# The first attention of a fused attention and gated-MLP kernel: division by the softmax sums after P times V instead of before

## The chip, the cores and the metric

One core of one Trainium2 chip runs the whole program. The metric is the device time of one execution in microseconds (us). The profile is of one execution; its time stands beside its span.

## What is computed

For 8 batches, 8 heads of width 64 and 576 positions: causal attention with a window of 128 positions and a bias that falls with distance, then a gated MLP whose second half is normalized and mixed along the sequence. Cut to what matters:

```python
scores = q @ k.T / 8;  rel = pos[:, None] - pos[None, :]
scores = where((rel >= 0) & (rel < 128), scores - slope[h] * abs(rel), -1e9)
p = exp(scores - max(scores));  attn = p / (sum(p) + 1e-9);  x = attn @ v
h = relu(x @ w_in);  u, g = halves(h);  g = layer_norm(g)
out = (u * (w_spatial @ g + b_spatial)) @ w_out
```

## The kernel before, in words

Two heads make a pair, so a batch has four pairs; 576 query positions make five tiles (t), the last of 64. Inputs are float32. Later batches split P and V into two f16 words and transpose P by DMA. The first 25 tiles, the "raw" ones (`RAW`: all four pairs of batch 0 and the first pair of batch 1), do everything in f32 on TensorE. This is the code that the change touches.

A raw tile goes through `raw_tile` and `raw_rest`: scores of both heads into PSUM (L508); bias, mask and row maximum on VectorE (L514, a custom operation and a read of its accumulator); Exp on ScalarE with the row sum taken by its accumulator (L519); the addition of 1e-9 and the reciprocal (L525, L526), once for two pairs in batch 0; P times reciprocal, one instruction a head, on ScalarE (L540) or VectorE (L541); transposes of P against an identity (L550); a copy from PSUM to `pq` (L281); and x, transposed, as V (64 columns of weights a head, one head in each half of the array) times moving P (L568). Its high f16 word is a copy (L281) and its low word a subtraction (L576), both into `xt`. V was scaled on GpSimd (L490), in place. A pair of batch 0 has the buffers `prob`, `pq` by its slot. `gated` then works on `xt`: v units (L765, L787), u units (L817), spatial mixing (L838), output (L864); its call `first(t)` weaves the raw tiles of batch 0 and the preparation of the weights (`words`, L298 to L314; `win_split`, L341 to L346) between its v units. The weight words pass through a buffer `wa` into `wx`.

No order is written by hand. `Plan.add` collects operations with an engine, a cost, a due time and the buffer parts that they read and write; `either` gives two engines to choose from. `Plan.order` simulates the five queues with these costs, sends each `either` to the engine that it expects to end it first, takes the earliest due time of what is ready, and so sets the order of every engine's queue. The hardware then runs each queue in that order, each instruction when its inputs are there. A change of costs or dependences in the raw tiles can thus reorder all queues.

Of the kernel before, what the change touches and what calls it, by code (L numbers as in the profile page):

```python
# [13 lines left out]
I32 = mybir.dt.int32  # L14
# [18 lines left out]
class Buf:  # L33
# [107 lines left out]
def attn_gmlp_kernel(ctx, tc, qk, v, w_in, w_spT, b_sp, w_out, outT):  # L141
# [83 lines left out]
    rstat = fixed([P, 8, 8], F32, "rstat")  # L225
# [5 lines left out]
    def xcols(x, a, c0, c1):  # L231
        return parts(x, c0, c1, 32, (a,))
# [55 lines left out]
    def words(src, n, x, due):  # L288


        a = plan.buf(work, "wa", 2, [P, DH], F32)
        low = lambda: src()[:, :, 0].bitcast(U32)
        high = lambda: src()[:, :, 1]
        ai, xi, xu = lambda: a().bitcast(I32), lambda: x().bitcast(I32), lambda: x().bitcast(U32)
        A, X, W = (a, 0), (x, 0), (src, 0)

        def f():
            nc.scalar.activation(a(), high().bitcast(F32), AF.Abs)  # L298
        plan.add("ACT", act(n), due, f, [W], [A])

        def f():
            nc.vector.tensor_scalar(a(), a(), TINY, CLAMP, ALU.max, ALU.min)
        plan.add("DVE", dve(n, True), due, f, [A], [A])

        def f():
            nc.vector.tensor_scalar(xi(), ai(), 0x07FFFFFF, 3, ALU.bitwise_and, ALU.logical_shift_left)
        plan.add("DVE", dve(n, True), due + 1, f, [A], [X])
# [166 lines left out]
    def values(b, due):  # L474
# [11 lines left out]

        for p in range(NP):
            if (b, p) in RAW:
                def f(p=p):
                    nc.gpsimd.tensor_scalar(vb()[:, p], vb()[:, p], am()[:, 5:6], None, ALU.mult)  # L490
                plan.add("POOL", 800, due + 9011 + p, f, [(vb, p), (am, 1)], [(vb, p)])
        return vb, am

    def raw_tile(b, p, t, raw, vb, xt, slot, due, sums=None):

        m, k0, k1 = min(P, S - t * P), max(0, (t - 1) * P), min(S, (t + 1) * P)
        n, c0 = k1 - k0, P if t == 0 else 0
# [11 lines left out]
        plan.add("PE", SWITCH // 2 + pe(*[4 * n]), due, f, [(raw, k) for k in range(k0 // P, t + 1)], [(sc[j], 0) for j in range(2)])
        for j in range(2):  # L510
            h = 2 * p + j

            def f(j=j, h=h):
                nc.vector.tensor_tensor_reduce(pr[j](), sc[j]()[:m, 0, :n], tabs[h]()[:m, c0:c0 + n], -0.125, 3e38,  # L514
                                               ALU.add, ALU.min, st(NM, j))
            plan.add("DVE", dve(n), due + 300, f, [(sc[j], 0), (tabs[h], 0)], cols[j] + [(rstat, row)])

            def f(j=j):
                nc.scalar.activation(pr[j](), pr[j](), AF.Exp, bias=st(NM, j), scale=-1.0, accum_out=st(SM, j))  # L519
# [11 lines left out]
    def raw_rest(b, p, t, vb, xt, slot, due, row):  # L531
# [46 lines left out]
        if t == NQ - 1:  # L578
            tail(xt, due + 2200)
# [397 lines left out]
```

## Time and profile before

| | |
|---|---|
| median of 3 runs (lowest to highest) | 603.81 us (602.73 to 604.26) |
| the profiled execution, its span | 603.51 us, 601.8 us |
| TensorE (PE) busy | 556.0 us, 92% |
| VectorE (DVE) busy | 510.3 us, 85% |
| ScalarE (ACT) busy | 432.9 us, 72% |
| GpSimd (POOL) busy | 61.3 us, 10% |
| mean DMA rate | 132 GB/s |

PEld is TensorE's loading of weights, which can overlap its matmuls; SPq is the queue that issues DMAs. Busy times by engine are the union of its instructions. A row names the source line, then what is written, an arrow, and what is read. A matmul in f32 shows as two records, a transpose as one.

### The profile page before, as it was taken

To read this page: it belongs to the slowest core of one execution; us is meant where nothing else is said; L and a number is where in the kernel's file an instruction comes from. 1 tells how busy PE (TensorE), PEld (TensorE's weight loads), DVE (VectorE), ACT (ScalarE), POOL (GpSimd) and SP (SyncE) were. 2 spreads that over 40 slices of the span, in tenths; PEclk is the share of its full clock that TensorE was granted. 3 is DMA by queue.
4 is the path that set the end of the run, shared out by engine and by line. 5 is a ranking of instruction groups with operands and counts; after the bars stand their busy time and mean duration, and the time that the engine had idled before them with its cause. 6 is when DMAs were issued, how large, how long until landed. Compare 5 with 4: busy or idle time off the path is not lost. (4 is left out here: it accounts for less than half of the span.)

```text
span 601.8 us, 14776 instructions
## 1 busy us (share of the span) xinstructions
PE 556.0 (92%) x5359; PEld 415.1 (69%) x5359; DVE 510.3 (85%) x1813; ACT 432.9 (72%) x1361; POOL 61.3 (10%) x113
## 2 busy tenths in 40 slices
PE   4567797998799999999999999999999999999997
PEld 2245454777558885788667876888578867896786
DVE  6979999999899799988998989989998899954640
ACT  5678988797888678868886888767985877743212
POOL 2501041100010101010011002000101001000100
PEclk9988878999999999999999999999999999999999
DMA  8930421189944584587856693568555654451002
GB/s 279 377 123 3 154 90 36 48 173 243 209 119 96 177 196 111 121 207 148 169 115 150 128 214 93 124 169 185 129 106 120 167 111 80 80 121 39 1 11 70
DMA packets 149997, 79.64 MB, mean 132 GB/s; under 512 B 129826, under 2 KB 140066, under 8 KB 149924
## 3 DMA queue, kind: packets, MB, share of 16 engines
q1 hardware_dynamic: 149924, 78.70, 54.1%
q8 instruction: 42, 0.69, 0.5%
q14 instruction: 31, 0.25, 0.1%
HBM read 37.13 MB, written 9.44 MB: 77 GB/s over the span
## 5 line engine op out<-in xcount | busy, mean ns | idle before, releaser
L621 ACT ACTIVATE prob<-prob,stat 128x256 f32<-128x256 f32 (+2 forms) x270 | 124.7, 465 | 27.3 <-DVE stat L615 27.3
L864 PE MATMUL m<-gs,wout 128*128 128x288 f32 x768 | 112.7, 301 | 7.0 <-DVE o L872 5.1
L838 PE MATMUL m<-wsp,vn 128*128 128x288 f16 x768 | 114.0, 287 | 0.1
L864 PEld LDWEIGHTS m<-gs,wout 128*128 128x128 f32 x768 | 103.9, 188 | 11.3 <-DVE o L872 5.9
L661 DVE SCALAR_TENSOR_TENSOR pq<-prob,stat,pq 128x128 f16<-128x128 f32 x270 | 106.7, 434 | 3.1 <-ACT pq L656 2.3
L656 ACT ACTIVATE pq<-prob,stat 128x128 f16<-128x128 f32 x270 | 105.1, 465 | 3.9 <-ACT prob L621 2.3
L817 PE MATMUL m<-xt,win 128*128 128x288 f16 x768 | 101.5, 288 | 0.5 <-ACT vt L285 0.4
L817 PEld LDWEIGHTS <-win 128*128 128x128 f16 x768 | 74.6, 98 | 23.9 <-issue 4.5
L765 PE MATMUL m<-win,xt 128*128 128x512 f16 x384 | 87.2, 384 | 1.0 <-DVE o L872 0.9
L838 PEld LDWEIGHTS <-vn 128*128 128x128 f16 x768 | 72.3, 98 | 22.5 <-issue 4.0
L615 DVE CUSTOM_DVE_ANT_0 prob<-s,tab 128x256 f32<-128x256 f32 (+2 forms) x222 | 74.0, 377 | 0.0
L765 PEld LDWEIGHTS <-xt 128*128 128x128 f16 x384 | 36.8, 99 | 45.0 <-issue 3.3
L735 POOL TENSOR_TENSOR st<-st,nhalf 128x1 f32<-128x1 f32 (+1 forms) x40 | 26.1, 654 | 356.1 <-DVE st L731 356.1
L621 ACT ACTIVATION_READ_ACCUMULATOR prob<-prob,stat 128x1 f32 (+1 forms) x270 | 51.0, 189 | 0.0
L871 ACT ACTIVATE o<-m,am 128x288 f32<-128x288 f32 x38 | 18.8, 499 | 41.5 <-PE m L864 26.2
L846 DVE TENSOR_TENSOR u<-m,u 128x288 f32<-128x288 f32 x64 | 28.7, 449 | 21.6 <-PE m L838 21.3
L700 PE MATMUL x<-pt,vh 128*64 128x256 f16 (+6 forms) x756 | 42.5, 229 | 2.0 <-DMA pt<-pq 2.0
L285 ACT ACTIVATE u<-m 128x288 f32<-128x288 f32 x51 | 20.4, 403 | 32.9 <-PE m L817 32.4
L604 PE MATMUL s<-qkraw 64*64 64x192 f32 (+2 forms) x876 | 40.6, 310 | 0.0
L700 PEld LDWEIGHTS <-vh 128*64 128x64 f16 x756 | 32.6, 110 | 9.6 <-issue 9.4
L700 PE MATMUL x<-pt,vl 128*64 128x256 f16 (+6 forms) x378 | 35.7, 228 | 0.0
L604 PEld LDWEIGHTS s<-qkraw 64*64 64x64 f32 x876 | 30.0, 133 | 6.4 <-issue 5.3
(151 smaller groups left out, 819.1 us busy)
## 6 DMA issues: line engine op xcount, KB each, us to landing
qkraw<-in_qk_dram SPq DMA_DIRECT2D x28, 576.0 KB, 4.2
vb<-in_v_dram SPq DMA_DIRECT2D x32, 320.0 KB, 4.7
out_dram<-o SPq DMA_DIRECT2D x64, 144.0 KB, 2.2
vn<-in_w_in_dram SPq DMA_DIRECT2D x8, 512.0 KB, 7.1
pt<-in_w_out_dram SPq DMA_DIRECT2D x4, 512.0 KB, 4.4
gs<-in_w_spT_dram SPq DMA_DIRECT2D x4, 288.0 KB, 6.6
qkraw<-in_qk_dram SPq DMA_DIRECT2D x3, 320.0 KB, 8.2
pt<-pq SPq DMA_TRANSPOSE x54, 4.7
```

The lines of the kernel that those rows point to most:

```text
L604: nc.tensor.matmul(sc[k][j]()[out, i, a - k0:z - k0], raw()[rows, 0, q:q + D], raw()[rows, 1, a:z], start=True, stop=True, skip_group_chec ...
L615: nc.vector.tensor_tensor_reduce(pt(), sc()[:m, i, :n], tabs[h]()[:m, c0:c0 + n], -0.125, 3e38, ALU.add, ALU.min, st()[:m, NM, j, t:t + 1])
L621: nc.scalar.activation(pt(), pt(), AF.Exp, bias=st()[:m, NM, j, t:t + 1], scale=-1.0, accum_out=st()[:m, SM, j, t:t + 1])
L656: nc.scalar.activation(pq[j]()[:m, 0, cs], prob[j]()[:m, cs], AF.Copy, scale=st()[:m, RC, j, t:t + 1])
L661: nc.vector.scalar_tensor_tensor(pq[j]()[:m, 1, cs], prob[j]()[:m, cs], st()[:m, RC, j, t:t + 1], pq[j]()[:m, 0, cs], ALU.mult, ALU.subtract)
L700: nc.tensor.matmul(xp()[j * D:(j + 1) * D, x0:x0 + n], l()[:, kt, j * D:(j + 1) * D], rhs[:, o:o + n], start=j not in seen, stop=False, sk ...
L735: nc.gpsimd.tensor_tensor(st()[:m, 11:12], st()[:m, 10:11], nhalf()[:m], ALU.pow)
L765: nc.tensor.matmul(pt(), xt[c]()[:, X0[a] + t * P:X0[a] + (t + 1) * P], win()[:, c, w, DH:DF], start=(n == 0), stop=(n == 3 * NC_ - 1))
L817: nc.tensor.matmul(pt()[:, :HS], win()[:, c, w, d * P:(d + 1) * P], xt[c]()[:, X0[a] + hf * HS:X0[a] + (hf + 1) * HS], start=(n == 0), sto ...
L838: nc.tensor.matmul(pt()[:, :HS], l, r, start=(n == 0), stop=(n == len(ops) - 1))
L846: nc.vector.tensor_tensor(u(), pt()[:, :HS], u(), ALU.mult)
L864: nc.tensor.matmul(pt()[:, :HS], wout()[:, d, w, e * P:(e + 1) * P], gs[d]()[:, a, :], start=(n == 0), stop=(n == 3 * ND - 1))
```

## The change

P is no longer scaled. Exp loses its accumulator. The unscaled P is transposed as before, but is then the weights of TensorE (128 columns, one head after the other), and the moving operand is V with a 65th column of ones, a new tile `vones` that GpSimd fills (L502, L504). So x comes out with queries along partitions, and its 65th column is the row sum. `raw_tiles` takes one pair or, in batch 0, two: it adds 1e-9 to the sums (L578), takes reciprocals (L579), multiplies x by them (L586), transposes x on TensorE (L591, one transpose a pair) into the PSUM tile that it came from, and copies and subtracts for both pairs at once (L291, L600). `xt` holds two pairs in each of three buffers instead of one in each of six. `wa` is gone: the absolute value of the weight words (L307) is written to `wx` directly.

```diff
     def words(src, n, x, due):
-        a = plan.buf(work, "wa", 2, [P, DH], F32)
...
+            nc.scalar.activation(x(), high().bitcast(F32), AF.Abs)
+        plan.add("ACT", act(n), due, f, [W], [X])
...
     def values(b, due):
-                    nc.gpsimd.tensor_scalar(vb()[:, p], vb()[:, p], am()[:, 5:6], None, ALU.mult)
+                vo = vones[p] = plan.buf(work, "vones", 4, [P, NQ, 2, D + 1], F32)
+                    nc.gpsimd.tensor_scalar(vo()[:, :, :, 0:D], vb()[:, p].rearrange("q a (j d) -> q a j d", j=2), am()[:, 5:6], None, ALU.mult)
+                plan.add("POOL", 150, due, lambda vo=vo: nc.gpsimd.memset(vo()[:, :, :, D:D + 1], 1.0), (), [(vo, 1)])
...
-    def raw_tile(b, p, t, raw, vb, xt, slot, due, sums=None):
+    def raw_tiles(b, t, raws, vos, xts, slots, due):
...
-                nc.scalar.activation(pr[j](), pr[j](), AF.Exp, bias=st(NM, j), scale=-1.0, accum_out=st(SM, j))
+                    nc.scalar.activation(pr(i, j), pr(i, j), AF.Exp, bias=nm(j), scale=-1.0)
...
-            plan.either([("ACT", act(n, 1), lambda j=j: nc.scalar.activation(pr[j](), pr[j](), AF.Copy, scale=st(RC, j))),
-                         ("DVE", dve(n, True), lambda j=j: nc.vector.tensor_scalar(pr[j](), pr[j](), st(RC, j), None, ALU.mult))],
...
-                    nc.tensor.matmul(xp()[j * D:(j + 1) * D, :m], vb()[:w, p, k // P, j * D:(j + 1) * D], pf(w, c, c + m),
+                        nc.tensor.matmul(xp()[:m, o:o + D + 1], pf(w, c, c + m), vos[i]()[:w, k_ // P, j, :],
...
+            nc.vector.tensor_scalar(TM(), xv()[:, :, D:D + 1], 1e-9, None, ALU.add)
+            nc.vector.reciprocal(RC(), TM())
+        plan.add("DVE", 220, due + 1900, f, XP, [(rstat, (row, 2))])
...
+            nc.vector.tensor_tensor(xn().rearrange("p (j d) -> p j d", j=J), xv()[:, :, 0:D], RC().to_broadcast([m, J, D]), ALU.mult)
+        plan.add("DVE", dve(J * D), due + 1950, f, XP + [(rstat, (row, 2))], ncols)
...
+                nc.tensor.transpose(xp()[:, i * m:(i + 1) * m], xn()[:, i * P:(i + 1) * P], ident()[:m, :m])
+        plan.add("PE", SWITCH // 2 + pe(*[2 * m] * len(raws)), due + 2000, f, ncols + [(ident, 0)], XP)
...
+        copy(len(raws) * m, lambda: (xt(0), xT()), due + 2100, XP, xh)
+            nc.vector.tensor_tensor(xt(1), xT(), xt(0), ALU.subtract)
...
-        xt = plan.buf(work, "xt", 6, [P, 2 * S + R], F16)
+            held[b, p // 2] = plan.buf(work, "xt", 3, [P, 2, 2 * S + R], F16)
```

TensorE's queue after the first tiles' transposes, before (x is the PSUM tile of P times V, s that of the scores, m that of the transposes):

```order
L568 MATMUL x<-pq_95,vb 64x128 x2
L508 MATMUL s_66<-qkraw 128x256
L508 MATMUL s_67<-qkraw 128x256
L568 MATMUL x<-pq_96,vb 64x128 x2
L568 MATMUL x<-pq_95,vb 64x128 x2
L508 MATMUL s_68<-pt 128x256
L508 MATMUL s_69<-pt 128x256
L568 MATMUL x<-pq_96,vb 64x128 x2
```

And the same place of the change:

```order
L568 MATMUL x<-vones,pq_95 128x65 x2
L568 MATMUL x<-vones,pq_96 128x65 x2
L568 MATMUL x<-vones,pq_95 128x65 x2
L568 MATMUL x<-vones,pq_96 128x65 x2
L591 MATMUL x<-ident,prob_93 128x128 x4
L526 MATMUL s_66<-qkraw 128x256
L526 MATMUL s_67<-qkraw 128x256
L526 MATMUL s_68<-pt 128x256
L526 MATMUL s_69<-pt 128x256
```

The scores of the second tile's pairs 2 and 3 stood between the x matmuls of the first tile; they now stand behind all of these and behind the transposes of x.

VectorE's queue in the change, over the same work (wx are the words of the weights; L586 and L600 are of pairs 0 and 1 of the first tile, L578 and L579 of pairs 2 and 3):

```order
L586 TENSOR_TENSOR prob_93<-x,rstat 128x256
L319 SCALAR_TENSOR_TENSOR wx<-vn_125,wx 128x512
L311 TENSOR_SCALAR wx<-wx 128x512
L323 SCALAR_TENSOR_TENSOR wx<-vn_125,wx 128x512
L315 TENSOR_SCALAR wx<-wx 128x512
L600 TENSOR_TENSOR xt<-x,xt 128x2x128
L319 SCALAR_TENSOR_TENSOR wx<-vn_129,wx 128x512
L311 TENSOR_SCALAR wx<-wx 128x512
L323 SCALAR_TENSOR_TENSOR wx<-vn_129,wx 128x512
L315 TENSOR_SCALAR wx<-wx 128x512
L578 TENSOR_SCALAR rstat<-x 128x4
L579 RECIPROCAL rstat<-rstat 128x4
```

The subtraction of pairs 0 and 1 (L600) now stands ahead of words of the weights and of the sums and the normalization of pairs 2 and 3; before, VectorE's only step on x was one subtraction a pair (L576).

## Rows read from the trace of the kernel before

**Rows 1.** The table of stages, over the whole span: start and end in us, length, then busy us (and instructions) of PE, PEld, DVE, ACT and POOL, the clock granted to TensorE as a share of 2.4 GHz, the DMA engines' busy share, GB/s.

```profile
0.00:45.00 45.00, 24.86 (x131) 14.70 (x132) 34.01 (x141) 29.74 (x96) 12.00 (x18) 0.95 0.73 261
45.00:105.00 60.00, 48.84 (x324) 29.11 (x323) 55.63 (x186) 52.77 (x150) 12.09 (x22) 0.83 0.22 71
105.00:150.00 45.00, 42.49 (x474) 32.87 (x472) 44.20 (x174) 36.39 (x127) 3.79 (x8) 1.00 0.67 152
150.00:300.00 150.00, 144.76 (x1530) 110.39 (x1531) 135.64 (x488) 119.53 (x386) 11.05 (x23) 1.00 0.70 157
300.00:450.00 150.00, 148.32 (x1543) 112.34 (x1542) 138.62 (x492) 118.57 (x378) 13.55 (x26) 1.00 0.64 142
450.00:560.00 110.00, 109.17 (x1073) 83.71 (x1071) 87.69 (x301) 68.56 (x213) 7.70 (x14) 1.00 0.45 98
560.00:602.00 42.00, 37.56 (x295) 31.98 (x293) 14.51 (x36) 7.37 (x16) 1.14 (x2) 0.98 0.09 29
```

**Rows 2.** What PE waited for between 45 and 105 us: waiting line, releaser, us in total, times, longest.

```profile
PE m L433 <- DVE wide L431: 3.4, 1, 3.4
PE s L550 <- ACT prob L540: 3.4, 1, 3.4
...
PE m L550 <- ACT prob L540: 3.0, 1, 3.0
```

**Rows 3.** The table of stages for three short stretches; columns as in rows 1.

```profile
45.00:47.50 2.50, 2.50 (x15) 2.17 (x16) 1.53 (x6) 1.41 (x4) 1.28 (x5) 0.50 0.07 13
...
77.50:80.00 2.50, 2.47 (x14) 1.71 (x14) 2.39 (x7) 1.78 (x5) 0.00 (x0) 0.50 0.07 13
...
97.50:120.00 22.50, 22.50 (x208) 16.40 (x207) 21.15 (x73) 16.94 (x55) 2.94 (x6) 0.97 0.20 55
```

**Rows 4.** Instructions by line and shape from 0 to 110 us: count, then busy us and mean ns of one, then idle time of the engine before them and what ended it.

```profile
L514 DVE CUSTOM_DVE_ANT_0 prob<-s,tab 128x256 f32<-128x256 f32 x30 | 11.8, 416 | 1.0 <-PE s L508 0.5 <-PE m L550 0.3
...
L519 ACT ACTIVATION_READ_ACCUMULATOR prob<-prob,rstat 128x1 f32 x40 | 7.6, 190 | 0.0
L540 ACT ACTIVATE prob<-prob,rstat 128x256 f32<-128x256 f32 x15 | 6.8, 497 | 0.8 <-DVE rstat L526 0.8
...
L576 DVE TENSOR_TENSOR xt<-x,xt 128x128 f16<-128x128 f32 x20 | 5.5, 281 | 1.8 <-ACT xt L281 1.8
...
L541 DVE TENSOR_SCALAR prob<-prob,rstat 128x256 f32<-128x256 f32 x15 | 4.4, 347 | 0.0
...
L281 DVE COPY pq<-m 128x512 f32<-128x512 f32 x4 | 2.7, 688 | 1.0 <-PE m L550 1.0
...
L541 DVE TENSOR_SCALAR prob<-prob,rstat 128x128 f32<-128x128 f32 x9 | 2.0, 281 | 0.1
...
L541 DVE TENSOR_SCALAR prob<-prob,rstat 64x192 f32<-64x192 f32 x6 | 1.5, 306 | 0.0
...
L525 DVE TENSOR_SCALAR rstat<-rstat 128x4 f32<-128x4 f32 x8 | 1.3, 167 | 3.0 <-ACT prob L519 3.0
...
L576 DVE TENSOR_TENSOR xt<-x,xt 128x64 f16<-128x64 f32 x4 | 0.8, 216 | 0.0
```

**Rows 5.** The timeline from 28 to 62 us: start, us, engine, line, operation, how many in a row.

```profile
28.36 0.40 DVE L514 CUSTOM_DVE_ANT_0 prob<-s,tab 128x256 f32<-128x256 f32 x1
...
30.90 0.51 ACT L519 ACTIVATE prob<-prob,rstat 128x256 f32<-128x256 f32 x1
...
31.41 0.50 ACT L519 ACTIVATE prob<-prob,rstat 128x256 f32<-128x256 f32 x1
...
34.78 1.09 PE L550 MATMUL m<-ident,prob 128*128 128x128 f32 x8
...
48.31 2.73 DVE L346 SCALAR_TENSOR_TENSOR win<-wx,ham,win 128x512 f16<-128x512 f32 x4
...
52.04 0.76 DVE L302 TENSOR_SCALAR wa<-wa 128x512 f32<-128x512 f32 x2
...
56.82 1.71 ACT L540 ACTIVATE prob<-prob,rstat 128x256 f32<-128x256 f32 x4 [0.51 <-DVE rstat L526]
```

**Rows 6.** The timeline of PE alone from 56 to 120 us.

```profile
57.38 2.10 PE L550 MATMUL m<-ident,prob 128*128 128x128 f32 x8 [3.04 <-ACT prob L540]
...
70.91 1.09 PE L568 MATMUL x<-pq,vb 128*64 128x128 f32 x16
...
107.69 0.54 PE L838 MATMUL m<-wsp,vn 128*128 128x288 f16 x3
```

**Rows 7.** The table of stages for line L568 alone: start and end, length, busy us (and records) of PE and PEld, granted clock, DMA share, GB/s.

```profile
45.00:105.00 60.00, 10.23 (x116) 6.86 (x116) 0.83 0.22 71
```

**Rows 8.** The chain that ended last, in order of time: start, us, engine, tile and line, records.

```profile
509.19 1.72 PE m L838 x14
```

**Rows 9.** The timeline from 0 to 45 us.

```profile
1.18 0.10 POOL L381 MEMSET wam<- 128x8 f32 x1
...
4.01 1.67 PE L508 MATMUL s<-qkraw 64*128 64x128 f32 x8 [4.01 <-DMA qkraw<-in_qk_dram]
...
16.62 8.44 POOL L490 TENSOR_SCALAR vb<-vb,am 128x640 f32<-128x640 f32 x4 [0.73 <-ACT pq L281]
...
19.31 1.23 PE L508 MATMUL s<-qkraw 64*128 64x256 f32 x4
...
23.72 1.23 PE L508 MATMUL s<-pt 64*128 64x256 f32 x4
```

More of the change, by code (lines that the diff above doesn't have):

```diff
@@ L509, in raw_tile @@
[L509 to L518, printed above, removed]
-                nc.scalar.activation(pr[j](), pr[j](), AF.Exp, bias=st(NM, j), scale=-1.0, accum_out=st(SM, j))
-            plan.add("ACT", act(n, 2), due + 600, f, cols[j] + [(rstat, row)], cols[j] + [(rstat, row)])
@@ L522, in raw_tile @@
-        r0, r1 = sums or (row, row + 1)
-        def f():
-            nc.vector.tensor_scalar(rstat()[:m, r0:r1, TM:TM + 2], rstat()[:m, r0:r1, SM:SM + 2], 1e-9, None, ALU.add)
-            nc.vector.reciprocal(rstat()[:m, r0:r1, RC:RC + 2], rstat()[:m, r0:r1, TM:TM + 2])
-        if sums is None or row == r1 - 1:
-            plan.add("DVE", 190, due + 900, f, [(rstat, r) for r in range(r0, r1)], [(rstat, r) for r in range(r0, r1)])
-        return lambda: raw_rest(b, p, t, vb, xt, slot, due, row)
@@ new lines, in raw_tiles @@
+        J = 2 * len(raws)
+        xv = lambda: xp()[:m, 0:J * (D + 1)].rearrange("p (j e) -> p j e", j=J)
+        XP = [(xp, i) for i in pairs]
+        TM, RC = [lambda c=c: rstat()[:m, row, c:c + J].rearrange("p (j o) -> p j o", o=1) for c in (4, 8)]
+        due += 1500 * (len(raws) - 1)
+        def f():
+            nc.vector.tensor_scalar(TM(), xv()[:, :, D:D + 1], 1e-9, None, ALU.add)
+            nc.vector.reciprocal(RC(), TM())
+        plan.add("DVE", 220, due + 1900, f, XP, [(rstat, (row, 2))])
@@ L578, in raw_rest @@
+        plan.add("DVE", dve(len(raws) * m), due + 2200, f, XP + xh, xl)
         if t == NQ - 1:
-            tail(xt, due + 2200)
+            for x in xts:
+                tail(x, due + 2300)
     def clear():
@@ L908, in attn_gmlp_kernel @@
     mixing_weights(FIRST + 8000)
-    x0 = [plan.buf(work, "xt", 6, [P, 2 * S + R], F16) for _ in range(NP)]
+    x0 = [xbuf(0, p) for p in range(NP)]
     wu = []
@@ L913, in first @@
         for p0 in range(0, NP, 2) if t < NQ else ():
[L914 to L916 removed]
+            raw_tiles(0, t, loads[p0:p0 + 2], [vones0[p] for p in (p0, p0 + 1)], x0[p0:p0 + 2], [p0, p0 + 1], 2000 + t * 6500 + p0 * 1500)
         if t == 1:
```

163 lines of the change are left out of this document (90 added, 73 removed).

## The prediction

> **What bounds the kernel now.** I read the table of stages first [rows 1]. From 150 us on TensorE (PE) is busy 439.8 of 452 us at a granted clock of 0.98 to 1.00, and the work there is not touched. The 25 tiles of the first attention (five of each of batch 0's four head pairs, five of batch 1's first pair) lie before 115 us. So a gain or a loss has to arise in the first 150 us, and it reaches the end only as far as PE then starts its long full stretch earlier or later. Before 45 us PE is idle 20.1 us, from 45 to 105 us 11.2 us, from 105 to 150 us 2.5 us. VectorE (DVE) is busy 55.6 of 60 us and then 44.2 of 45: from 45 to 150 us it is the engine with the least room, 95%, while ScalarE (ACT) has 52.8 of 60 and 36.4 of 45.
>
> The waits of PE between 45 and 105 us come second [rows 2]: 6.4 us in two waits of the transposes L550 for the scaling L540 on ACT, and 3.4 us for the small matmul L433, whose input is queued on DVE behind ACT's work. Third comes the clock [rows 3]: after such idle time PE runs at 1.2 GHz (0.50), and from 97.5 to 120 us it is busy all the time at 0.97 of 2.4 GHz. Whatever is added on PE there has no cover.
>
> **Part by part: DVE.** Fifty scalings of P by the reciprocal go. The table by shape [rows 4] has 30 of them on DVE, 4.4 + 2.0 + 1.5 = 7.9 us, and the order of the instructions shows that 30 stood on DVE and 20 on ACT. The 25 subtractions L576 (20 of 281 ns, 5 of 216 ns: 6.7 us) become 15 for two pairs or one. Ten of these have two pairs: eight have 256 elements and two 128; five have one pair, four of 128 and one of 64. For 256 elements from PSUM the nearest row is L514 at 416 ns, so 8 x 0.42 + 6 x 0.28 + 0.22 = 5.3 us: 1.4 us less. New are 15 normalizations L586, ten of 256 elements and five of 128: 10 x 0.42 + 5 x 0.28 = 5.6 us more. The addition and the reciprocal keep their count of 15, but the addition now reads four scattered PSUM words; bounds are 0 (as L525's 167 ns) and 0.25 us each (as L514's 416 ns); I take 0.05, 0.8 us. The planner, which sees less work on ACT, also moves shared operations off DVE: two P copies (688 ns each, 1.4 us) and six small casts late in batch 0, for which I take 1.2 us: 288 of the 512 elements that cost 688 ns would make 2.3 us, and 0 is the other end, as they may be off the path. A relu leaves DVE and a weight split comes to it, which cancel. Sum for DVE: -7.9 - 1.4 + 5.6 + 0.8 - 2.6 = **-5.5 us**.
>
> **ACT.** Twenty scalings go (15 of them 6.8 us). Fifty reads of the accumulator go too; 40 are booked with 7.6 us, but they overlap: two Exp with a read start 0.51 us apart, four L540 of the same shape take 1.71 us, 0.43 each [rows 5], so a read costs 0.08 us and fifty cost 4. Pair casts replace single ones (about -3), two P copies come (+1.2). ACT loses some 14 us. It isn't the bound after 45 us, so I count nothing for it beyond what it does to waits: the 3.0 us that DVE's L525 waited for Exp [rows 4] go, since the sums now come from PE. In their place L578 and L586 wait for P times V; I let these cancel, with ends of -3 and +3.
>
> **PE.** The trace has no f32 matmul with 128 columns of weights and 65 moving. Now eight matmuls of two tiles (16 records, two a matmul) take 1.09 us [rows 6], 0.136 us each, two heads side by side in the array's halves. The heads now follow each other. Nearest for a full f32 load is the transpose L550: 1.09 us for eight records at full clock [rows 5], 0.136 us a record, 2.10 us at half clock [rows 6]. Two records make 0.27 us a matmul at full clock and 0.53 at half; the other bound is 0.136, if loads hide. I take 0.27, so 0.136 more a matmul, and 0.136 for each new transpose of x; at half clock it is twice that. From 45 to 105 us run 116 of L568's 180 records, 58 of 90 matmuls [rows 7]. Twenty of them, of the last query tile, load 64 columns and count half, so 48, and with some 14 transposes 62 x 0.136 = 8.4 us at full clock against 11.2 us of idle time: hidden if it falls into that idle time, and I count it so. Behind 97.5 us the last three tiles of batch 1 run on a full PE: two with five instructions and one of half that, 12.5 x 0.136 = **+1.7 us**, not hidden.
>
> The Trainium skill, page "TensorE: Matmul & The Clock Gate", section "Part 3: Packing small matmuls", says that weight loads overlap matmuls in flight only when their row groups differ; these are all full-height. By that each of 180 records would also pay for streaming its 65 columns, at least 27 ns, 4.9 us more on PE, and the slow rival below would be likelier. The trace disagrees for f16: 14 full-height matmuls of 288 columns take 1.72 us [rows 8], 123 ns each, about their columns alone, so loads are hidden there. No row shows it for f32 with so few columns.
>
> **The first tile's queue.** Before, PE computed scores for pairs 2 and 3 of the second tile at 19.31 and 23.72 us, between the x matmuls that wait for POOL's four scalings of V (16.62 to 25.06 us) [rows 9]. Now those scores stand behind all four x and behind the transposes of x. The second transpose needs a DVE normalization that itself is queued behind the subtraction of pairs 0 and 1, hence behind the first transpose, hence behind the last V: I trace the scores to about 30 us and their softmax, which DVE began at 28.36 us [rows 5], to some 2 us later. Against that, POOL starts about 0.8 us earlier (six reads and a scaling less on ACT's path to the scale of V), and ACT saves five scalings and 16 reads, 3.5 us, on its way to what L433 waits for. I take 0 at 45 us, with ends -2 and +2.
>
> **At no cost.** POOL's memsets of the ones column (0.10 us each, as L381) come before the mask tables, but the first scores wait for their load until 4.01 us [rows 9]. The V loads of batch 2 move from SP's later queue to right behind the w_in loads, since V's buffer is free once POOL has written the new tile; DMA is busy 22% after 45 us [rows 1], which covers them; if it did not, batch 1's Q and K loads behind them would be late next. Without its own buffer the first step of the weight words waits until the split has freed the target (L346, 48.31 to 51.04 us); DVE only comes to those words at 52.04 us [rows 5]. If that cover goes, one ACT and one DVE step, about 1.1 us, is late once.
>
> **Sum.** The profiled execution took 603.51 us (span 601.8, and 1.7 around it), 0.3 below the median of 603.81. 603.5 - 5.5 (DVE) + 1.7 (PE, uncovered) + 0 = **599.7 us**.
>
> **Rivals.**
> 1. *Everything shows.* PE's transposes no longer wait for sums, reciprocal and scaling, the added PE work falls into idle time, and DVE's 3.0 us of waiting for Exp go without replacement: 603.5 - 5.5 - 3.0 = 595.0. For it: the 6.4 us of PE waits on L540. Against: PE full from 97.5 us.
> 2. *Hidden.* PE's backlog takes it: 8.4 us more in a stretch with 11.2 us idle leaves 2.8 us; where steps that depend on each other can't use more than half of the 11.2 us, 2.8 us stay uncovered, and with the 1.7 they use up most of the 5.5: 603.5 - 5.5 + 2.8 + 1.7 = 602.5. For it: 100% PE from 97.5 to 120 us.
> 3. *Slower: PE becomes the bound between 45 and 105 us.* Place: the f32 loads at L568. It decides from 11.2 / 62 = 0.18 us more an instruction. At half clock the price is 0.27, 16.8 us in all, 5.6 more than the idle time; with the 1.7 behind it and no gain from DVE, which then waits for PE, 603.5 + 5.6 + 1.7 = 610.8. Midway between no loss and that, 607. For it: 45 to 47.5 and 77.5 to 80 us run at 0.50 [rows 3], and PE now also waits in order for DVE's normalization 15 times. Against: fewer long waits should leave less half clock.
>
> **How the numbers follow.** Forecast (gain of 2 to 6 us) 0.36; rival 1 0.14; rival 2 0.20; rival 3 0.30. About 0.3%, 1.8 us, is what a measurement of this kernel can tell from no change: faster 0.50, same 0.20, slower 0.30. The range runs from 594.5 (just past rival 1) to 608 (most of rival 3): the dear end of rival 3 and a gain above rival 1 are left out. The forecast's own range is 597.5 to 602.
>
> **What would show it.** Right: L541, L540 and the reads gone, DVE's busy time 0 to 150 us down by about 5 us, L568 at about 0.27 us a matmul at full clock, PE idle from 45 to 105 us below 5 us, and the first matmuls of the spatial mixing (L838 before) 2 to 5 us earlier than 107.69 us [rows 6]. Wrong: an L568 matmul above 0.4 us, or PE waiting long for L586, or a first stage that reaches 45 us' work 3 us late. Were the time moved by what happens after 150 us, the whole argument would be wrong.

## The result and the profile after

The changed kernel takes **607.65 us** (median of 20 runs) where the kernel before, beside it, takes 603.57: ratio 1.0063, 95% interval 1.0048 to 1.0079, **slower by 3.8 us**. The forecast was 599.7. A second batch gave 607.36, ratio 1.0066 (1.0037 to 1.0096). Medians are over all runs; the ratios leave out disturbed ones.

The profiled execution took 603.19 us, the shortest of its 20, so a second trace was taken in the first experiment, of an execution of 608.68 us. I call them the short and the typical one, though the latter is 1 us above the median. Table of stages of the short execution (columns as in [rows 1]):

```profile
0.00:45.00 45.00, 25.70 (x137) 18.42 (x137) 28.12 (x112) 26.16 (x64) 12.17 (x22) 1.00 0.80 290
45.00:105.00 60.00, 54.55 (x374) 37.63 (x375) 55.38 (x190) 45.73 (x110) 12.60 (x25) 0.89 0.16 51
...
150.00:300.00 150.00, 147.00 (x1555) 112.96 (x1554) 134.47 (x484) 119.97 (x386) 12.91 (x23) 1.00 0.70 155
...
sum 602.00, PE 561.68 PEld 426.86 DVE 502.32 ACT 424.77 POOL 62.05; mean PE 80.24 PEld 60.98 DVE 71.76 ACT 60.68 POOL 8.86
```

The same of the typical execution:

```profile
0.00:45.00 45.00, 25.70 (x129) 18.36 (x129) 27.69 (x110) 23.86 (x59) 12.14 (x22) 1.00 0.80 290
45.00:105.00 60.00, 52.34 (x305) 35.80 (x306) 49.62 (x173) 44.17 (x106) 10.45 (x22) 0.80 0.13 40
...
sum 607.00, PE 564.79 PEld 429.74 DVE 502.34 ACT 424.41 POOL 61.66; mean PE 80.68 PEld 61.39 DVE 71.76 ACT 60.63 POOL 8.81
```

Set the second rows beside each other: in the same 60 us the typical execution got through 305 PE records at a clock of 0.80, the short one through 374 at 0.89. DVE is relieved as forecast, and more (510.29 to 502.34 us). PE's idle time over the span fell only from 45.8 us (601.8 - 556.0) to 42.2 (607.0 - 564.8). PE's busy time rose by 8.8 us. If busy time times one less the granted clock, in 3 us windows from 27 to 132 us, is taken as what the half clock cost, that is 9.0 us before, 7.6 in the short and 10.1 in the typical execution; the rest is work at full clock: 547.0 before, 554.1 and 554.7 after. So the change added 7 to 8 us of PE work and took 3.6 us of idle time off a typical execution (6 off the short one), while what the half clock costs in all rose by only 1.1 us.

Where [rows 4 and 7] stood, the short execution has these groups, of PE from 45 to 105 us:

```profile
L568 PE MATMUL x<-vones,pq 128*128 128x65 f32 (+2 forms) x132 | 19.4, 284 | 2.5 <-POOL vones L502 1.4 <-DVE xt L600 0.9 <-ACT pq L291 0.2
L591 PE MATMUL x<-ident,prob 128*128 128x128 f32 (+1 forms) x16 | 3.7, 297 | 1.5 <-DVE prob L586 1.5
```

and of DVE from 0 to 125 us:

```profile
L586 DVE TENSOR_TENSOR prob<-x,rstat 128x256 f32<-128x256 f32 (+3 forms) x15 | 5.5, 369 | 0.2
L600 DVE TENSOR_TENSOR xt<-x,xt 128x256 f16<-128x256 f32 (+2 forms) x15 | 5.1, 346 | 1.1 <-ACT xt L291 1.1
L578 DVE TENSOR_SCALAR rstat<-x 128x4 f32<-128x4 f32 (+3 forms) x15 | 2.3, 153 | 5.3 <-PE x L568 5.2
```

L541 and L540 are gone, and so are the reads. The place that matters is in the PE timeline of the typical execution, around the small matmul of the first w_in split (L433 before, now L442); in brackets the idle time ahead and what ended it:

```profile
14.57 0.26 PE L442 MATMUL m<-wide,ones 128*128 128x128 bf16 x1 [3.64 <-DVE wide L440]
...
31.50 1.23 PE L526 MATMUL s<-qkraw 64*128 64x256 f32 x4 [0.25 <-DVE rstat L532]
32.52 1.06 PE L526 MATMUL s<-pt 64*128 64x256 f32 x4
...
38.17 1.94 PE L568 MATMUL x<-vones,pq 128*128 128x65 f32 x16
...
42.37 0.70 PE L526 MATMUL s<-qkraw 64*128 64x256 f32 x4
42.91 0.60 PE L526 MATMUL s<-pt 64*128 64x256 f32 x4
...
48.55 0.29 PE L442 MATMUL m<-wide,ones 128*128 128x128 bf16 x1 [2.25 <-DVE wide L440]
48.63 1.91 PE L551 MATMUL m<-ident,prob 128*128 128x128 f32 x8
50.42 1.97 PE L568 MATMUL x<-vones,pq 128*128 128x65 f32 x8
...
53.04 3.51 PE L568 MATMUL x<-vones,pq 128*128 128x65 f32 x16
...
57.20 4.61 PE L795 MATMUL m<-win,xt 128*128 128x512 f16 x12
```

The kernel before reached that matmul at 44.88 us, 30.3 us behind its first small matmul (14.56); here it is 34.0 us (48.55 - 14.57): **3.7 us late**, in the short execution 2.6. What follows runs at half clock: 16 records of L568 take 3.51 us, against 1.94 at 38.17 us. Why the matmul is late stands on the timeline of ACT, typical execution,

```profile
43.84 0.67 ACT L397 ACTIVATE wsp<-gs 128x576 f16<-128x576 f32 x1
44.41 0.19 ACT L397 ACTIVATION_READ_ACCUMULATOR wsp<-gs 128x1 f32 x1
44.51 1.69 ACT L537 ACTIVATE prob<-prob,rstat 128x256 f32<-128x256 f32 x4
46.10 0.67 ACT L401 ACTIVATE r<-gs 128x576 f16<-128x576 f32 x1
...
46.88 0.68 ACT L402 ACTIVATE r<-gs 1x576 f16<-1x576 f32 x1
```

and on that of DVE:

```profile
47.69 0.16 DVE L448 TENSOR_REDUCE wam<-wam 128x1 f32<-128x6 f32 x1 [2.23 <-ACT r L402]
...
48.21 0.29 DVE L440 TENSOR_SCALAR wide<-ident,ham 128x128 bf16<-128x128 f32 x1
```

DVE's L440, which PE waits for, is queued behind L448, which waits for ACT's two last sums of the spatial weights (L401, L402); and those are queued behind four Exps of the third tile, whose scores PE computed at 42.37 and 42.91 us.

The order at this place is not new. In the kernel before, the same two sums (L392, L393) also stood behind 24 Exps, those of the first three tiles. But there the last scores of the third tile came 6.6 and 5.4 us earlier, on PE,

```profile
35.81 0.70 PE L508 MATMUL s<-qkraw 64*128 64x256 f32 x4
...
37.52 0.70 PE L508 MATMUL s<-pt 64*128 64x256 f32 x4
...
44.88 0.29 PE L433 MATMUL m<-wide,ones 128*128 128x128 bf16 x1 [3.42 <-DVE wide L431]
...
49.49 2.75 PE L765 MATMUL m<-win,xt 128*128 128x512 f16 x12
```

and so the last of the 24 Exps on ACT, and the sums behind it, came earlier too:

```profile
41.27 0.49 ACT L519 ACTIVATE prob<-prob,rstat 128x256 f32<-128x256 f32 x1
...
42.43 0.67 ACT L392 ACTIVATE r<-gs 128x576 f16<-128x576 f32 x1
...
43.21 0.68 ACT L393 ACTIVATE r<-gs 1x576 f16<-1x576 f32 x1
```

PE began the first twelve records of a v unit (L765, now L795) at 49.49 us before, and at 57.20 us in the typical execution (52.61 in the short one).

### The profile page after: what moved, and what is told of

Same layout as the page of the kernel before. It is cut to its first block, busy times and chain, and to the rows that moved or that the text cites. A ratio compares the mean times of both kernels' runs of the same rounds, so it can differ in the third digit from the quotient of the medians.

```text
span 601.5 us, 14726 instructions
## 1 busy us (share of the span) xinstructions
PE 561.7 (93%) x5384; PEld 426.9 (71%) x5384; DVE 502.3 (84%) x1779; ACT 424.8 (71%) x1290; POOL 62.1 (10%) x118
## 5 line engine op out<-in xcount | busy, mean ns | idle before, releaser
L894 PE MATMUL m<-gs,wout 128*128 128x288 f32 x768 | 110.9, 299 | 5.0 <-DVE o L902 3.3
L795 PE MATMUL m<-win,xt 128*128 128x512 f16 x384 | 87.8, 385 | 0.1
L795 PEld LDWEIGHTS <-xt 128*128 128x128 f16 x384 | 36.9, 99 | 44.2 <-issue 3.1
L765 POOL TENSOR_TENSOR st<-st,nhalf 128x1 f32<-128x1 f32 (+1 forms) x40 | 27.6, 690 | 323.1 <-DVE st L761 314.7
L901 ACT ACTIVATE o<-m,am 128x288 f32<-128x288 f32 x44 | 21.9, 499 | 40.5 <-PE m L894 26.5
L295 ACT ACTIVATE u<-m 128x288 f32<-128x288 f32 x51 | 20.6, 404 | 31.5 <-PE m L847 30.9
L730 PE MATMUL x<-pt,vh 128*64 128x256 f16 (+6 forms) x756 | 42.2, 229 | 0.3 <-DMA pt<-pq 0.2
L629 PE MATMUL s<-qkraw 64*64 64x192 f32 (+2 forms) x876 | 40.6, 310 | 0.4 <-DVE stat L640 0.4
L629 PEld LDWEIGHTS s<-qkraw 64*64 64x64 f32 x876 | 29.9, 133 | 7.2 <-issue 6.2
```

The lines of the kernel that those rows point to most:

```text
L629: nc.tensor.matmul(sc[k][j]()[out, i, a - k0:z - k0], raw()[rows, 0, q:q + D], raw()[rows, 1, a:z], start=True, stop=True, skip_group_chec ...
L730: nc.tensor.matmul(xp()[j * D:(j + 1) * D, x0:x0 + n], l()[:, kt, j * D:(j + 1) * D], rhs[:, o:o + n], start=j not in seen, stop=False, sk ...
L765: nc.gpsimd.tensor_tensor(st()[:m, 11:12], st()[:m, 10:11], nhalf()[:m], ALU.pow)
L795: nc.tensor.matmul(pt(), xt[c]()[:, X0[a] + t * P:X0[a] + (t + 1) * P], win()[:, c, w, DH:DF], start=(n == 0), stop=(n == 3 * NC_ - 1))
L894: nc.tensor.matmul(pt()[:, :HS], wout()[:, d, w, e * P:(e + 1) * P], gs[d]()[:, a, :], start=(n == 0), stop=(n == 3 * ND - 1))
```

## The experiments

Beside each ratio the table has three numbers of the kernel's trace, which is of a single execution: when PE reached that small matmul, the idle time ahead of it, and the granted clock from 45 to 60 us. Names of two or three parts combine the edits of those parts.

| run | us | ratio to before (95%) | reached | idle | clock |
|---|---|---|---|---|---|
| before | 603.6 | | 44.88 | 3.42 | 0.84 |
| after_again | 607.36 | 1.0066 (1.0037-1.0096) | 48.55 | 2.25 | 0.58 |
| after_late | 610.76 | 1.0123 (1.0095-1.0150) | 43.91 | 1.07 | 0.67 |
| after_single | 604.34 | 1.0037 (1.0009-1.0064) | 45.50 | 2.38 | 0.77 |
| after_twice | 627.70 | 1.0411 (1.0377-1.0445) | 49.88 | 1.77 | 0.69 |
| after_f16 | 603.16 | 0.9997 (0.9981-1.0013) | 45.87 | 1.45 | 0.74 |
| after_vact | 605.28 | 1.0025 (1.0010-1.0041) | 41.76 | 0 | 1.00 |
| single_vact | 607.48 | 1.0054 (1.0027-1.0081) | 45.31 | 2.47 | 0.69 |
| after_warm | 604.41 | 1.0023 (0.9996-1.0050) | 46.31 | 0.35 | 1.00 |
| before_sub2 | 609.59 | 1.0092 (1.0067-1.0117) | 46.83 | 3.63 | 0.80 |
| after_sub2 | 612.21 | 1.0146 (1.0122-1.0171) | 48.40 | 1.79 | 0.57 |
| before_twice | 609.89 | 1.0100 (1.0074-1.0127) | 45.87 | 3.63 | 0.84 |
| before_warm | 603.56 | 0.9994 (0.9980-1.0009) | 44.08 | 0 | 0.89 |
| single_vact_warm | 605.01 | 1.0002 (0.9970-1.0033) | 43.25 | 0.58 | 1.00 |
| vact_all | 598.77 | 0.9910 (0.9887-0.9933) | 42.01 | 0 | 1.00 |
| f16_vact_all | 597.44 | 0.9897 (0.9866-0.9928) | 40.63 | 0 | 1.00 |
| before_vact | 606.27 | 1.0036 (1.0017-1.0056) | 42.88 | 2.31 | 0.84 |
| v_order | 601.07 | 0.9952 (0.9937-0.9967) | 44.44 | 0 | 1.00 |
| vact_b1 | 607.57 | 1.0054 (1.0036-1.0073) | 48.22 | 2.25 | 0.56 |

**What differs between executions.** after_again is the changed kernel without an edit.

> The changed kernel once more, to have the trace of a second execution of it; the profiled one (603.2 us, granted clock 0.986 over the span) was the shortest of its 20 runs, whose median is 607.65 us. Theory 1 (the granted clock differs between executions: PE has more places where it runs dry before 130 us, and what follows them runs at half clock or not): the trace of a longer execution has a lower mean clock (0.975 to 0.983), the lost 3 to 5 us lie before 150 us, and PE's busy time there is 3 to 6 us larger with the same instructions. Theory 2 (the first tile's queue takes longer in most executions, by a DMA or by POOL): the first x matmuls or the scores behind them start 2 us or more later than at 30.3 and 31.3 us, and the clock is the same. Theory 3 (the loss lies behind 150 us, in DMA transfers of the later batches): the first stage ends as in the first trace and PE has new waits behind 150 us. Median again near 607 us.

As theory 1 has it: clock 0.980 over the span, the loss before 150 us, PE's busy time 3.1 us larger. But of the 5.5 us between the two spans only 2.5 are half clock by the sum above; 2.4 are idle time. Theory 2 falls short (scores 1.2 us later than in the short execution, not 2, and its first small matmul, at 13.38 us, also was 1.2 us earlier). PE's idle time from 150 to 300 us is the same, 3.0 and 3.1 us, so theory 3 falls.

**What more work on one engine costs.** Doubling shows how much cover an engine has, that is, idle time that can take more work.

```diff
 # after_twice (L568); before_twice repeats its x matmuls over the first result
+for again in range(2):
     for k, (k_, w) in enumerate(blocks): ...
 # before_sub2 (L576) and after_sub2 (L600)
+for _ in range(2):
     nc.vector.tensor_tensor(xt(1), xT(), xt(0), ALU.subtract)
```

> The changed kernel with every matmul of P times V issued twice into the same accumulation: x and the sums both double, and the quotient stays. This adds 90 matmuls with 128 columns of f32 weights and 65 moving columns, at 0.24 us each at full clock some 20 us of PE before 120 us. PE price theory (the added 5.7 us of PE work is what the change lost): nearly all of it shows, +15 to +22 us, and the same share of the 5.7 us, 4 to 6 us, is the loss of the change. Queue theory (PE has room before 105 us, and waits for others): less than half shows, +3 to +9 us. Clock theory: more work on PE means fewer dry spots, so the granted clock before 150 us rises and part of the price comes back: +3 to +12 us.

> The kernel before with every x matmul (L568) issued twice, the second time over the first's result: 90 more matmuls of two heads' halves at 0.136 us at full clock, 12.2 us of PE. The same doubling added 20.3 us to the changed kernel, all of its price at full clock. Theory A (DVE set the time before, PE had cover): at most half shows, +2 to +6 us. Theory B (both together): +6 to +10. Theory C (PE's work set the time before as after): +10 to +14 us.

> The kernel before with every subtraction of the first attention on DVE (L576) issued twice with the same operands and result: 25 more DVE instructions, 6.7 us of DVE time before 115 us. Theory A (DVE was what set the end of the first stage, as the prediction had it): nearly all of it shows, +5 to +7 us. Theory B (PE and DVE together, each waiting for the other, so that work taken from one alone gives little): +2 to +5 us. Theory C (PE's work and clock set it, DVE has cover): under +2 us.

> The changed kernel with its 15 subtractions L600 issued twice, 5.3 us more of DVE time before 115 us: the counterpart on the changed kernel. Theory A' (after the change DVE still sets the end): +4 to +5.5 us over 607.4. Theory B (both engines together): +1.5 to +4. Theory C' (the change has made PE the bound, DVE's relief is cover now): under +1.5 us. If the kernel before loses 5 us or more by the same edit and this one under 1.5, the bound has moved from DVE to PE.

On the changed kernel the added PE work cost 20.3 us, its full price; on the one before 6.2 of 12.2 us, half (the two traces show 10.7 us more work at full clock). So PE has less cover than before, as theory B of before_twice and the price theory of after_twice had it; but the interval of before_twice, 4.5 to 7.7 us, reaches into its theory A, and the smaller dose is the easier one to hide. DVE's added work costs nearly all on both: 5.9 us more for 6.4 before (theory A), 4.8 for 5.3 after (theory A'). The bound has not moved from DVE to PE: with the change both are on the path, in turn. Added DVE time thus costs some nine tenths of itself; that DVE time taken off is worth as much, as the forecast had it, was not shown.

**The price of the f32 loads.**

```diff
 # after_f16
-vo = ... plan.buf(work, "vones", 4, [P, NQ, 2, D + 1], F32)
+vo = ... plan.buf(work, "vones", 4, [P, NQ, 2, D + 1], F16)
-pf = ... pq[slot % 2]() ... .bitcast(F32)[:w, a0 + x0:a0 + x1]
+pf = ... pq[slot % 2]() ... [:w, 2 * a0 + x0:2 * a0 + x1]
```

> The changed kernel with P and the tile of V and ones held in f16 for the x matmuls of the first attention (x then comes from rounded P and V; the rest of the computation stays). Each of the 90 matmuls is one record with an f16 load in place of two records with f32 loads; chains, waits and the order of the instructions stay as they are. PE price theory (what the change lost is the f32 load of 128 columns that each x matmul needs): PE's busy time falls by at least 12 us before 125 us (from 0.24 to about 0.1 us a matmul, twice that at half clock), and the time falls from 607.4 to 592 to 598, below the kernel before. Queue theory (first tile's V, normalization and transposes set the time): 604 to 607. Clock theory (dry spots of PE cost half clock behind them, however short the matmuls): less PE work makes the dry spots longer, so half-clock time stays or grows; 600 to 604.

The x matmuls of after_f16 from 45 to 105 us:

```profile
L568 PE MATMUL x<-vones,pq 128*128 128x65 f16 (+1 forms) x66 | 7.4, 215 | 4.2 <-POOL vones L502 2.2 <-DVE xt L600 1.1 <-ACT pq L291 0.7
```

Half the records, 7.4 us in place of 19.4, and 4.2 us off the time, level with the kernel before. Both the price theory (592 to 598) and the queue theory (604 to 607) miss; the clock theory's 600 to 604 is hit. PE's busy time fell by 11 us against the typical execution (553.6, span 603.2), and its idle time rose to 49.6: taking PE work away gives back about a third of it. That DVE then sets the pace is likely, but was not tried.

**The first tile's queue.**

```diff
 # after_late: late for tile 0 of batch 0 only, POOL's 2090 for all five scalings
+late = 12000 if b == 0 and t == 0 else 0      # added to the dues of x, sums, L586, L591, cast, L600
-plan.add("POOL", 800, due + 9011 + p, f, ...)
+plan.add("POOL", 2090, due + 9011 + p, f, ...)
 # after_single: batch 0
-raw_tiles(0, t, loads[p0:p0 + 2], ...)
+for p in (p0, p0 + 1): raw_tiles(0, t, [loads[p]], ...)
 # after_vact, for b == 0; vact_b1, for b == 1; vact_all and before_vact (there in place), for both
-nc.gpsimd.tensor_scalar(vo()..., vb()..., am()[:, 5:6], None, ALU.mult)
-plan.add("POOL", 800, ...)
+nc.scalar.activation(vo()..., vb()..., AF.Copy, scale=am()[:, 5:6])
+plan.add("ACT", 700, ...)
```

> The changed kernel, in which only the planner's numbers for the first query tile of batch 0 differ: the scaling of V is booked with the 2,090 ns that POOL takes, and x, the sums, the normalization and the transpose back of that tile come due 12 us later. The scores of the second tile then stand ahead of what waits for POOL. Queue theory (the scores of the second tile stand behind x and its transposes, start at 30 us in place of 19 to 24, and all behind them is late): the scores come before 26 us, the first stage ends 2 to 4 us earlier, and the time falls from 607.6 to about 604. PE price theory (f32 loads of 128 columns make PE the bound from 45 to 105 us): no more than 1 us, 606.5 to 608. Clock theory (waits followed by half clock): between, as far as the long waits go; 604 to 607.

> The changed kernel with batch 0's tiles taken one pair at a time, as it takes batch 1's first pair: 25 chains of sums, reciprocal, normalization, transpose, cast and subtraction in place of 15, but no pair waits for the other one. Coupling theory (x, sums and transposes of two pairs in one PSUM tile make the first pair wait for the second): the waits of the transposes for the normalization (5.5 us before 150 us) fall, and the time is 2 to 4 us below 607.6. Other theories (queue, PE price, clock): DVE gets about 10 more normalizations, sums and subtractions, some 5 us before 105 us, PE's work stays; 608 to 612.

> The changed kernel with the four scalings of batch 0's V on ACT (which idles from 20 to 26 us) in place of POOL, some 0.7 us each in place of 2.1. The waits of PE for POOL (6 to 7 us before 26 us) and with them the 4.0 us of the second transpose for DVE shrink. Queue theory: the scores of the second tile come 3 us or more earlier than at 30.3 to 31.5 us, and the time falls by 3 to 5 us to 602 to 604. PE price theory with full PE from 31 us on: what is won at 31 us ends up as dry time or half clock before 130 us, and no more than 1.5 us reaches the end: 605.5 to 607.5.

> Both edits together: batch 0's tiles one pair at a time, and V scaled on ACT. Single pairs alone gave 604.3 us, 3 us below the changed kernel. If both act on the same thing (the first tile's queue, which single pairs also shorten: scores at 29.2 us there), this gives the better of the two alone, 602 to 604.5. If they act on different things, the gains add: 599 to 601.5, below the kernel before. If PE's work and clock set the time alone: 604 to 606.

after_late brought the second tile's scores to 26.79 us and the small matmul to 43.91, and lost: 610.8. All theories miss. Its PE ran at half clock from 41 to 55 and from 72 to 86 us (14.2 us lost by the sum used above). An earlier queue alone is no gain. The median of after_single is 3.0 us lower, but its runs fall into two groups (eight at 602.6 to 604.8 us, four at 608.8 to 609.1), its interval overlaps that of after_again, and its transposes still waited 4.5 us for L586 (5.5 in the short execution); so coupling isn't shown, though it predicted the time. after_vact gained 2.1, just outside both ranges. Both together gained nothing: no theory. Ordered by the clock from 45 to 60 us (0.67, 0.69, 0.77, 1.00) the four took 610.8, 607.5, 604.3 and 605.3 us. This is no strict order, but it led to the next three runs.

**Half clock.** after_warm puts 32 matmuls whose result is overwritten into the idle time ahead of L442; before_warm does so at L433, single_vact_warm in the combination.

```diff
+for _ in range(32):
+    nc.tensor.matmul(pt()[:, :P], ones(), ones(), start=True, stop=True)
 nc.tensor.matmul(pt()[:, :P], ones(), wide()[:, 0, :], start=True, stop=True)
```

> The changed kernel with 32 idle bf16 matmuls (ones times ones, 128 columns, into the PSUM tile that the next matmul overwrites) on PE just ahead of the small matmul of the first w_in split, where PE waited 2.3 to 2.5 us for DVE in front of the half-clock stretch at 48 us. They fill that wait, and add about 2 us of PE work where there is none. Clock theory (the dry spot ahead of 48 us sets off half clock, for 3 us in one execution and 15 us in the other): the granted clock from 48 to 63 us is 0.9 to 1.0 in most executions, the spread of the runs shrinks, and the time falls by 3 to 5 us to 602.5 to 604.5. If half clock comes from elsewhere (earlier dry spots, or the kind of work behind): 607 to 609, the filler costing 0 to 2 us.

> The kernel before with the same 32 idle matmuls ahead of the small matmul of the first w_in split, where PE waited 3.4 us before 44.9 us. On the changed kernel they took the time from 607.4 to 604.4 us. If the changed kernel loses more half clock than the one before does (the clock is part of what the change cost): under 1.5 us gain here. If both kernels lose alike to the dry spot: -2 to -4 us, 599.5 to 601.5, and the filler's gain is no part of the change's loss.

> Single pairs in batch 0, V of batch 0 scaled on ACT, and the 32 idle matmuls ahead of the first w_in split's small matmul, where PE waited 2.47 us before 45.3 us. Single pairs alone gave 604.3, V on ACT alone 605.3, both together 607.5 with PE at half clock from 45 to 54 us, 72 to 84 and 99 to 105. Clock theory (the gains of the two edits were taken back by half clock behind that dry spot): full clock from 46 us, and 601 to 604. If the two edits hinder each other otherwise (order, DVE's extra 5 us): 606 to 609.

PE of after_warm, to be set beside the typical execution:

```profile
43.99 1.96 PE L445 MATMUL m<-ones 128*128 128x128 bf16 x32
46.31 0.22 PE L446 MATMUL m<-wide,ones 128*128 128x128 bf16 x1 [0.35 <-DVE wide L440]
46.36 1.26 PE L556 MATMUL m<-ident,prob 128*128 128x128 f32 x8
...
49.08 2.00 PE L573 MATMUL x<-vones,pq 128*128 128x65 f32 x16
```

The matmul is no earlier than in the short execution, and nothing waits less, but 16 records take 2.00 us, not 3.51. The time fell by 3.0 us, and eleven of twelve runs lie between 603.5 and 605.3 (18 of 20 of the changed kernel: 603.2 to 609.8). The kernel before gains nothing: its PE falls to half clock earlier, from 39 us, so the same edit is no equal test there. So half clock behind this idle spot costs the changed kernel about 3 us. That these are the change's own isn't shown: the kernel before lost 9.0 us to half clock in all, the typical execution 10.1. In single_vact_warm the clock is 1.00 too, but it gains 2.5 us to 605.0, not to below 604: its expectation is missed by 1 us, and the interval to the kernel before holds 1.

**The order.** A planner that books V on ACT writes another order, so two things change at once. v_order separates them: planned as vact_all, hence the same order on every engine, but the scaling issued on POOL.

```diff
 # v_order
 nc.gpsimd.tensor_scalar(vo()..., vb()..., am()[:, 5:6], None, ALU.mult)
-plan.add("POOL", 800, due + 9011 + p, f, ...)
+plan.add("ACT", 700, due + 9011 + p, f, ...)
```

> The changed kernel with all five scalings of V on ACT, that of batch 1's first pair too, for which PE waits 2.5 us around 90 us (6 to 9 us after the dry spot at half clock). V of batch 0 alone on ACT gave 605.3. Queue theory with a second place in batch 1: another 1 to 2.5 us, 603 to 604.5. Otherwise 605 to 606, PE then waiting for the exponentials or DVE at that place.

> All five scalings of V on ACT, and P and V in f16 for the x matmuls. f16 alone gave 603.2 (4.2 below the changed kernel), V of batch 0 on ACT 605.3 (2.1 below). If the two take away different parts of the loss (PE's f32 loads; the first tile's wait for V), the sum: 600 to 602, faster than the kernel before. If both only feed dry spots that DVE and the clock set: 603 to 604.

> The control: the kernel before with its five scalings of V on ACT (in place, as on POOL before). If the changed kernel suffers from POOL's V more than the one before (there, scores of the second tile filled PE's waits for POOL): within 1 us of 603.6. If V on ACT is a gain for either kernel alike: 601 to 602.5, and it explains nothing of the change's loss.

> The order of the kernel with all scalings of V on ACT (598.8 us), word for word on every engine, but the five scalings issued on POOL after all, in the place where that order has them: planned as 0.7 us on ACT, run as 2.1 us on POOL. Order theory (the loss of the changed kernel is where its planner puts x, scores and batch 1's scale, not how long V takes): 598.5 to 601. Duration theory (PE waits for POOL's V, 8.4 us for batch 0 and 2.1 for batch 1, and dry spots with half clock follow): 603.5 to 608.

> Only the scaling for batch 1's first pair on ACT, batch 0's four left on POOL. Batch 0's alone on ACT gave 605.3, all five 598.8. If batch 1's place is worth 6.5 us by itself: 600 to 602. If the first tile's V has to come early for it to count (the later place then being reached earlier): 604.5 to 607.

The timeline of PE of v_order at the same place, and then that of ACT:

```profile
43.38 1.14 PE L526 MATMUL s<-qkraw 64*128 64x256 f32 x8 [1.26 <-DVE rstat L532]
44.44 0.23 PE L442 MATMUL m<-wide,ones 128*128 128x128 bf16 x1
44.53 1.24 PE L551 MATMUL m<-ident,prob 128*128 128x128 f32 x8
45.89 1.11 PE L568 MATMUL x<-vones,pq 128*128 128x65 f32 x8
...
47.28 2.00 PE L568 MATMUL x<-vones,pq 128*128 128x65 f32 x16
...
49.56 2.75 PE L795 MATMUL m<-win,xt 128*128 128x512 f16 x12
```

```profile
41.32 0.67 ACT L401 ACTIVATE r<-gs 128x576 f16<-128x576 f32 x1
...
42.10 0.68 ACT L402 ACTIVATE r<-gs 1x576 f16<-1x576 f32 x1
...
42.90 1.82 ACT L537 ACTIVATE prob<-prob,rstat 128x256 f32<-128x256 f32 x4
```

The scores of the second tile come no earlier than in the changed kernel (30.65 us), and POOL's scaling still takes 2 us a pair. But the weight sums on ACT now stand ahead of the four Exps, behind 20 in place of 24, as in neither of the two kernels (DVE's L448 starts at 43.57 us, 4.1 earlier, 0.8 of it because this execution's first small matmul came at 13.79 us). The small matmul comes without idle time, PE stays at full clock, and the first v unit begins level with the kernel before. The work at full clock is that of the changed kernel, 554.4 us by the sum above; half clock costs 5.5 us and PE idles 39.2. The order theory has it: 601.07, 0.07 past its upper end, **6.3 us off the changed kernel and 0.5% faster than the kernel before**. The order differs in other places too, among them POOL's scale of batch 1's V. In the typical execution of the changed kernel:

```profile
87.56 0.23 POOL L461 TENSOR_SCALAR ham<-ham 128x1 f32<-128x1 f32 x1 [6.86 <-DVE st L760]
...
89.14 0.56 POOL L461 TENSOR_SCALAR am<-am 128x1 f32<-128x1 f32 x1
...
90.53 2.07 POOL L502 TENSOR_SCALAR vones<-vb,am 128x640 f32<-128x640 f32 x1
```

and in v_order:

```profile
78.65 1.46 POOL L461 TENSOR_SCALAR am<-am 128x1 f32<-128x1 f32 x1 [5.79 <-DVE am L452]
...
82.42 1.92 POOL L502 TENSOR_SCALAR vones<-vb,am 128x640 f32<-128x640 f32 x1
...
88.03 0.85 POOL L461 TENSOR_SCALAR ham<-ham 128x1 f32<-128x1 f32 x1 [1.60 <-ACT vn L291]
```

There V waits behind the scale of w_in's second half, and PE waited 2.5 us for it at 92.66 us. vact_b1 put that one scaling on ACT without moving the scale ahead, and gained nothing (its second theory, missed by 0.6 us). vact_all passed its range (598.8; 603 to 604.5 expected), 2.3 us below v_order: that is what V's duration is worth. f16_vact_all is the fastest, below the 600 to 602 expected, but it rounds P and V. before_vact lost 2.9 us where 0 or a gain was expected, so V on ACT is no gain by itself, or its new order takes it back.

Against the typical execution most of v_order's gain stands ahead of the second place: its first v unit begins 7.6 us earlier, and the whole execution took 7.8 us less (600.86 against 608.68). But later places count as well. after_vact and vact_all have the same order on PE, ACT and DVE up to 78 us and still lie 6.5 us apart; from 150 to 300 us PE idles 6.8 us in after_vact and 3.0 in vact_all. How the 6.3 us divide over the places was not separated. Nor was an order like v_order's, with the sums ahead of the four Exps, tried on the kernel before; so the runs show that another order takes the loss away, and not that the change is a gain at an equally good order.

## Why the prediction was wrong

**The step that failed** is the first tile's queue, "I take 0 at 45 us, with ends -2 and +2". The scores came at 30.3 to 31.5 us, as traced there. The set-off did not come: "ACT saves ... 3.5 us, on its way to what L433 waits for". ACT had the time, but the two last weight sums stand behind 24 Exps, as they did before, and the last of these ended at 46.2 us in place of 41.8, since the third tile's scores were late as well. So what L433 waited for came 2.6 to 3.7 us later. I followed the lateness up to the second tile's softmax, and not through the third tile on DVE and ACT, where the chain runs. The prediction's own sign for it ("a first stage that reaches 45 us' work 3 us late") is what the trace shows.

**DVE, -5.5 us**: right in kind, too small: -8.0. L586 5.5 us (5.6 forecast), L600 1.4 below L576, but L578 costs nothing extra from PSUM (153 ns), and what the planner moved off DVE is some 4 us, not 2.6. This relief did not reach the end of the typical execution; after_sub2 and before_sub2 show only that added DVE time costs nine tenths of itself.

**PE's price**: right: 0.242 us a matmul at full clock (1.94 us for 16 records at 38.17 us), 0.27 forecast; at half clock 0.44. The Trainium skill (page "TensorE: Matmul & The Clock Gate", section "Part 3: Packing small matmuls") says that weight loads overlap matmuls in flight only when their row groups differ; with the 65 columns paid on top, the estimate worked out from that is 0.33 us. The traces do not bear it out: eight records with 65 moving columns take 1.11 us (v_order at 45.89 us), eight transposes with 128 take 1.09 [rows 5], so no price of the columns shows. **That 8.4 us of it hide in 11.2 us of idle time** was wrong: PE got 7.7 us more work, and its idle time over the span fell by only 3.6 us in the typical execution; from 45 to 105 us it fell to 5.5 (short) and 7.7 us, not below 5. Part of the price was paid at half clock, and after_twice found no cover left. Without the f32 loads the change is even (after_f16). v_order does the same work in 7.9 us less span (4.6 less half clock, 3.0 less idle time), so in another order the cover was there.

**The waits** did not cancel. PE's 6.4 us for L540 [rows 2] became 1.5 for L586, but DVE's L578 waits 5.2 us for L568 where L525 waited 3.0 [rows 4], and the 3.4 us in front of the small matmul [rows 2] stayed as 2.2, later and ahead of heavier PE work.

**Rival 3** (607, chance 0.30) named the side and the size, and half of the mechanism: the loads at half clock at L568. Not in it was the idle spot ahead of L442, behind which that half clock stands. PE did not become the bound from 45 to 105 us: it idled 5.5 to 7.7 us there. By its own sum for full clock (0.18 us more an instruction needed, 0.11 found) it should not have come about; that its 607 fits is in part luck.

**The forecast's sum** for the edited arithmetic is not refuted: with another order and the same instructions v_order took 601.1, inside the forecast's own range of 597.5 to 602. It isn't confirmed either, since that order also moves the four Exps out of the way, which stood there before the change too. Rival 1 (595.0) was reached by none of the runs in f32.

**A sign that misled:** the first matmul of the spatial mixing came at 113.08 us (119.74 in the typical execution), not ahead of 107.69. But in v_order it comes at 112.75, and that kernel is faster: the planner now puts batch 1's scores (L629) first. A milestone of a re-planned kernel is no clock.

## What to carry to other kernels

A change that moves one dependency in a planned kernel re-plans every in-order queue. Follow the chain that PE waits for on every engine, down to the last sum, in times and not in order alone, before a wait is called even: here the sums stood behind the same Exps as before, and the Exps came later; planning as one kernel and issuing as another separates order from cost. And when work is added where PE has idle time, ask whether it lies behind an idle spot: it may then be paid at half clock, as here at 53 us.

## What the runs showed of the hardware

Around the same idle time of 2.25 us the half clock lasted about 3 us in the short execution and some 13 in the typical one, PE being busy from the small matmul on. Two windows of the short execution, with the granted clock third from the end:

```profile
47.50:50.00 2.50, 2.50 (x14) 2.39 (x13) 2.22 (x6) 1.85 (x4) 1.17 (x4) 0.50 0.01 0
50.00:52.50 2.50, 2.50 (x23) 2.50 (x22) 2.46 (x7) 1.16 (x2) 0.00 (x0) 0.90 0.00 0
```

and one of the typical:

```profile
45.00:60.00 15.00, 12.58 (x56) 10.03 (x57) 9.66 (x30) 7.49 (x17) 1.34 (x5) 0.58 0.01 2
```

Half clock in all makes 2.5 of the 5.5 us between the two executions; why it lasts so unequally no run showed. It isn't the only thing that spreads the times: six executions of single_vact had the same clock over the span, 0.989, and took from 603.0 to 609.5 us. No trace here shows what differs in those.

Scaling one pair's V and writing it into the tile with the ones took ACT 0.82 us (five of them 3.8 us together) and POOL 2.10.
